# Twelve more weight pieces rounded during attention, the second of an iteration between its halves

## The chip, the cores and the metric

One Trainium2 chip, one core. The metric is the device time of one execution in microseconds (us).

## The reference, cut to what matters

Three layers follow each other: attention with a sigmoid in place of softmax, a mixture of eight experts with one expert for each token, and a gated layer. All of it is float32.

```python
scores = q @ k.T / sqrt(64) - log(448)          # batch 4, 12 heads, 448 tokens, 64 wide
x = sigmoid(scores) @ v                         # -> x [1792, 768]
e = argmax over 8 experts of the logits of x    # gate_w: softmax weight of that expert
x = gate_w * (relu(x @ w1[e]) @ w2[e])          # w1 [8, 768, 1024], w2 [8, 1024, 768]
out = ((x @ w_a) * (x @ w_b)) @ w_out           # 768 -> 1536 -> 768
```

The weights `w_a`, `w_b` and `w_out` of the last layer arrive as float64. The kernel reads each number as two 32-bit words and makes a float32 of them.

## The kernel before

**Precision.** TensorE multiplies in a form that keeps fewer bits than float32, so each operand is split into a high part (a ScalarE cast, L728) and a low part (a VectorE subtraction, L729), and each product takes three matmuls (L1035 to L1037, L1068 to L1070).

**The pieces.** The float64 weights are cut into 72 units (L163): 12 blocks `f` of 128 columns of the middle dimension, three parts (`w_a`, `w_b`, `w_out`), two halves. One unit is 128 x 384 numbers. `prep_load` (L171) issues on the SP queue the load of a unit into a buffer `raw`, of which there are four. `prep_unit` (L185) makes, on VectorE, the upper bits in `m` (L195, L197; two or three buffers), on ScalarE a float of the low word in `raw` itself (L199) and the absolute value of the top 16 bits in `ab` (L201; three buffers), and on GpSimd the sum (L202). `prep_finish` (L205) makes on VectorE the finished number (L212), in `ab` or, in the last layer, in place in the weight buffer. `prep_store` (L221) stores finished units on the SP queue: from `ab` into a scratch tensor `wm` in DRAM (L224).

**The tick.** `prep_tick(dma, behind)` (L226) does one step of this pipeline: store all that is finished, finish all pending units but `behind`, load the unit three ahead, begin the next unit.

**Attention** (L465) has 24 pairs of heads, one for each iteration `i` of the loop at L590 (and one iteration more to drain). In an iteration TensorE transposes q and k of pair i+1 (L515), computes the first half of the scores of pair i (L535, two PSUM buffers), half of the product with v of pair i-1 (L547), the second half of the scores, the second half of the product, and transposes the result of pair i-2 (`x_tok`, L563). ScalarE copies the transposes (L521) and applies the sigmoid from each PSUM buffer (L536). VectorE makes low parts (L522), copies results (L551, L564) and squares (L568). SP issues the loads of q, k (L500) and v (L495) for later pairs near the top of an iteration, and after every third `x_tok` the store of token rows `xs` (L573). In places of the loop `pump` lets the routing of finished batches go on (tables, flags). When the flags of the first half are known, `first_expert` (L794) loads and splits the first expert's weights, one slab in an iteration (L799).

The order on each engine is the order in which the program issues (`manual_schedule`, L1127): every engine and the SP queue work in order, and nothing overtakes. A buffer is given to the next user only when all readers of the former one are done; for `ab` the reader is the store.

Iterations 0 to 2 load a unit each; from iteration 3 on a tick stands at the end of each iteration, and a second one right behind it at iterations 9, 15 and 21: 21 + 3 = 24 units, the blocks 0 to 3 (`F_EARLY = 4`, L164). One of them is stored only in the layer behind, where `first_loads` (L702) drains the pipeline.

**The mixture of experts** (to about 546 us) holds no unit but that drain.

**The last layer** (`glu`, L950) takes the 1792 tokens in groups of 4, 4, 4 and 2 tiles of 128, and for each group goes through the 12 blocks: 48 steps. In a step it splits the weights of the next step (`w_split`, L995), makes both products of the block (`ab`, L1026), copies the first from PSUM (L1040), multiplies (L1043), splits the result, and issues the output matmuls (L1049) of the step before. `w_load` (L982) brings the three parts of a block, 1152 KB, back from `wm` two steps ahead; the blocks from `F_EARLY` on are not loaded in the first group, since `prep_more` (L1084) rounds their units there in place: one tick at the head of a step, one (even steps) or two (odd steps) between its two products, two at its end, as long as the block of the unit is at most 5 ahead of the step (L1088). 48 units are rounded there. At the end of step 1 the tokens of the next group are loaded (L1121).

Of the kernel before, what the change touches and what calls it, by code (L numbers as in the profile page):

```python
# [24 lines left out]
def build(ctx: ExitStack, tc: tile.TileContext, q, k, v, emb, tau, w1, w2, wa, wb, wo, out, dbg=None, stop=None):  # L25
# [6 lines left out]
    nc = tc.nc  # L32
# [128 lines left out]

    HU = DM // 2
    units = [(f, part, hf) for f in range(NF) for part in range(3) for hf in range(2)]  # L163
    F_EARLY = 4  # L164
    next_unit, unit_end = [0], [6 * F_EARLY]
    prep_raw = {}

# [3 lines left out]
    def prep_load(u, dma=nc.sync):  # L171
        if u >= unit_end[0]:
            return
        f, part, hf = units[u]
        t = prep_p.tile([P, HU, 2], I32, tag="raw", name="raw", bufs=4)
        if part < 2:
            src = (wa, wb)[part].bitcast(I32).rearrange("(k p) c -> p k c", p=P)
            dma.dma_start(out=t.rearrange("p (k c) t -> p k (c t)", k=KD // 2),
                          in_=src[:, hf * (KD // 2):(hf + 1) * (KD // 2), 2 * f * P:2 * (f + 1) * P])
        else:  # L180
            src = wo.bitcast(I32).rearrange("(f p) c -> p f c", p=P)
            dma.dma_start(out=t.rearrange("p n t -> p (n t)"), in_=src[:, f, 2 * hf * HU:2 * (hf + 1) * HU])
        prep_raw[u] = t

    def prep_unit():  # L185

        u = next_unit[0]
        if u not in prep_raw:
            return
        next_unit[0] += 1  # L190
        t = prep_raw.pop(u)
        top, low = t[:, :, 1], t[:, :, 0]
        t16 = t.rearrange("p n t -> p (n t)").bitcast(BF16).rearrange("p (n t) -> p n t", t=4)[:, :, 3]
        m = m3[0] if m3 and u % 3 == 2 else prep_p.tile([P, HU], I32, tag="m", name="m", bufs=2)
        nc.vector.tensor_scalar(out=m, in0=top, scalar1=3, scalar2=0x3FFFFFFF,  # L195
                                op0=ALU.logical_shift_left, op1=ALU.bitwise_and)
        nc.vector.scalar_tensor_tensor(out=m, in0=top, scalar=-0x40000000, in1=m,  # L197
                                       op0=ALU.bitwise_and, op1=ALU.bitwise_or)
        nc.scalar.activation(out=low, in_=low.bitcast(U32), func=AF.Copy, scale=2.0 ** -29)  # L199
        ab = prep_p.tile([P, HU], F32, tag="ab", name="ab", bufs=3)  # L200
        nc.scalar.activation(out=ab, in_=t16, func=AF.Abs)  # L201
        nc.gpsimd.tensor_tensor(out=m, in0=m, in1=low, op=ALU.add)  # L202
        prep_sum.append((u, m, ab))

    def prep_finish(behind=0):  # L205

        while len(prep_sum) > behind:
            u, m, ab = prep_sum.pop(0)
            f, part, hf = units[u]
            cs = slice(hf * HU, (hf + 1) * HU)  # L210
            to = wr[f][:, part, cs] if f in wr else ab
            nc.vector.scalar_tensor_tensor(out=to, in0=ab, scalar=1.125 * 2.0 ** -15, in1=m.bitcast(F32),  # L212
                                           op0=ALU.is_ge, op1=ALU.mult)
            if f not in wr:
                prep_out.append((wm_d[f][:, part, cs], ab))
                continue
            wr_n[f] = wr_n.get(f, 0) + 1
            if wr_n[f] == 6:
                prep_out.append((wm_d[f], wr[f]))

    def prep_store(dma=nc.sync):  # L221
        while prep_out:
            o, t = prep_out.pop(0)
            dma.dma_start(out=o, in_=t)  # L224

    def prep_tick(dma=nc.sync, behind=0):  # L226
        prep_store(dma)
        prep_finish(behind)
        prep_load(next_unit[0] + 3, dma)
        prep_unit()  # L230
# [220 lines left out]
    def pump(ps=(True, LATE, END)):  # L451

        while bg:
            job = next((j for j in bg if j[2]), bg[0])
            if job[1] and job[1] not in ps:
                return
            job[2] = False
            try:
                job[1] = next(job[0])
                return  # L460
            except StopIteration:
                bg.remove(job)


    def attention():  # L465
# [16 lines left out]
        NPR = len(pairs)  # L482
# [20 lines left out]
        def tr_pair(i):  # L503

            if i == 1:
                pt = [p.tile([P, 512], F32, tag=t, name=t) for p, t in ((ps_a, "av"), (ps_m, "pm"))]
                parts = [(pt[s][:, :S], slice(s, s + 1)) for s in range(2)]
            else:
                both = ps_t.tile([P, 2, 512], F32, tag="pt", name="pt")
                pt = [both[:, s] for s in range(2)]  # L510
                parts = [(both[:, :, :S], slice(0, 2))]
            for s, nm in enumerate(("q", "k")):
                t = raw.pop((i, nm))
                for c in range(NCH):
                    nc.tensor.transpose(out=pt[s][:, c * CP:(c + 1) * CP], in_=t[:, c].rearrange("p h d -> p (h d)"),  # L515
                                        identity=ident[:CP, :CP])
            hi = qk_p.tile([P, 2, S], F32R, tag="qkh", name="qkh")
            lo = qk_p.tile([P, 2, S], F32R, tag="qkl", name="qkl")
            for src, ss in parts:
                h, l = (t[:, ss, :] if src.ndim == 3 else t[:, ss.start, :] for t in (hi, lo))  # L520
                nc.scalar.copy(out=h, in_=src)  # L521
                nc.vector.tensor_tensor(out=l, in0=src, in1=h.bitcast(F32), op=ALU.subtract)  # L522
            QK[i] = (hi, lo)
# [52 lines left out]
        def routed(b):  # L576
            bg.append([route(b), True, True])
            if b == PHASES[phase_of[b]][-1]:
                bg.append([tables(phase_of[b]), False, False])
# [10 lines left out]
        for i in range(NPR + 1):  # L590
            if 0 < i and i + 1 < NPR:
                tr_pair(i + 1)
            load(i + 3, "qk")
            load(i + 2, "v")
            if i < NPR:
                score_half(i, 0)
            if i == NPR:
                one, turn = misc["ps"], [0]

                def either():  # L600
                    turn[0] ^= 1
                    return ps_s.tile([P, 2, 512], F32, tag="ps", name="pm2")[:, 0] if turn[0] else one()

                misc["ps"] = either
            pump((True,))
            if early_w is None and misc.get("flags0"):
                early_w = first_expert()
            if misc.get("tables0") and not misc.get("gathered"):
                gather(0)
                misc["gathered"] = True  # L610
            if early_w:
                early_w.pop(0)()
            if 1 <= i <= NPR:
                av_part(i - 1, 0)
            pump((True,))
            if i < NPR:
                score_half(i, 1)
            pump((LATE,))
            if 1 <= i <= NPR:
                av_part(i - 1, 1)  # L620
            if i == NPR:
                both = ps_s.tile([P, 2, 512], F32, tag="ps", name="px0")
                x_load(0, [both[:, hf] for hf in range(2)])
                gather(1)
            if i >= 2:
                x_tok(i - 2)
                b, hp = pairs[i - 2]
                if hp == NP - 1:
                    routed(b)
            if i < 3:  # L630
                prep_load(i)
            elif i < NPR:
                prep_tick(nc.sync)
                if i % 6 == 3 and i > 3:
                    prep_tick(nc.sync, 1)
            pump((END,))

        while early_w:
# [155 lines left out]
    def first_expert():  # L794
        e_of[0] = value(0, 2, E - 1, [ET.SP])

        def load(kk):
            if kk < KD:
                nc.sync.dma_start(out=r1[0][:, kk % 2, :], in_=w1[e_of[0], kk * P:(kk + 1) * P, :])  # L799

        def step(kk):
            split(w1h[kk], w1l[kk], r1[0][:, kk % 2, :], w1h[kk].bitcast(F32))
            load(kk + 2)

        load(0)
        load(1)
        return [lambda: None] + [(lambda kk=kk: step(kk)) for kk in range(KD)]
# [142 lines left out]
    def glu():  # L950
# [31 lines left out]
        def w_load(i):  # L982

            if i < len(steps):
                t = w_raw(i)
                if F_EARLY <= i < NF:
                    wraw[i] = [(s, slice(0, DM), t[:, s, :]) for s in range(3)]
# [7 lines left out]
        def w_split(i, parts=range(3), eng=nc.vector):  # L995
            if i < len(steps):
                if parts[0] == 0:
                    wsp[i] = [ws_p.tile([P, 3, DM], F32R, tag=nm, name=nm) for nm in ("whi", "wlo")]
                while F_EARLY <= i < NF and wr_n.get(i, 0) < 6:
                    prep_tick()  # L1000
# [170 lines left out]
```

## Time and profile before

| | us |
|---|---|
| median of three runs | 1116.95 |
| lowest and highest | 1114.82, 1117.33 |
| the profiled execution | 1113.61 |
| its span (first to last instruction) | 1111.9 |
| attention, first score to last product with v | about 10 to 206 |
| last layer, from its first transpose | 546 to 1112 |

The profile is one execution. Busy times are unions of an engine's instructions; TensorE's matmuls are pipelined and overlap. "Idle before" is an engine's gap ahead of an instruction, with the engine or transfer that ended it. PE is TensorE, PEld its weight load, DVE is VectorE, ACT is ScalarE, POOL is GpSimd and SP the queue that issues transfers.

### The profile page before, as it was taken

The numbers are of one execution on the slowest core, as the hardware profiler recorded it, in microseconds if no ns is written. First come the engines' busy times: TensorE is split into PE (matmuls) and PEld (weight loads), VectorE is DVE, ScalarE is ACT, GpSimd is POOL, SyncE is SP. The second block draws the span as 40 slices with busy tenths as digits, with TensorE's granted clock in tenths as the row PEclk, the third lists the DMA queues.
The fourth block names the chain that finished last, engine by engine and source line by source line (L and its number), as shares of the span: only waits on it lengthen the run. The fifth ranks groups of instructions, "written<-read, shape, count | busy, mean of one in ns | idle before, by whom it ended". The sixth has DMA issues, their size and how long they took to land.

```text
span 1111.9 us, 16742 instructions
## 1 busy us (share of the span) xinstructions
PE 1070.6 (96%) x5996; PEld 870.6 (78%) x5996; DVE 603.3 (54%) x1037; ACT 500.3 (45%) x761; POOL 178.2 (16%) x218
## 2 busy tenths in 40 slices
PE   7999999999999999999798889899999999999998
PEld 4555555599989898989787677788888888888997
DVE  2556688864853585352287998643333343333553
ACT  5766767431743474431355556333323232223442
POOL 2121322231221222121123343200000000000000
PEclk9999999999999999999899999999999999999999
DMA  9478586436644775331368566545231072220730
GB/s 201 138 199 214 150 231 197 165 106 266 230 185 169 270 263 192 136 136 45 106 216 278 173 211 214 198 155 214 91 122 43 4 295 103 110 86 1 310 131 29
DMA packets 108681, 182.98 MB, mean 165 GB/s; under 512 B 49560, under 2 KB 80792, under 8 KB 102560
## 3 DMA queue, kind: packets, MB, share of 16 engines
q1 hardware_dynamic: 104608, 166.54, 44.7%
q0 software_dynamic: 3040, 14.94, 3.8%
q8 instruction: 49, 0.80, 0.3%
q14 instruction: 56, 0.46, 0.1%
q10 hardware_dynamic: 928, 0.23, 0.1%
HBM read 149.45 MB, written 32.24 MB: 163 GB/s over the span
## 4 chain that ended last, share of the span: by engine, by line
PE 36%; DVE 9%; DMA 3%; issue 2%; ACT 1%; POOLq 0%; POOL 0%; SPq 0%; ACTq 0%; DVEq 0%
PE ab L1035 8%; PE ab L1037 8%; PE ab L1036 8%; PE o L1068 4%; PE o L1069 4%; PE o L1070 4%; DVE wlo L729 3%; DVE m L195 2%; DVE m L197 1%; DVE wx L212 1%; DMA r<-wm 1%; DMA yg<-ys 1%; DVE r L212 1%; DVE m L1043 1%; DVE gl L729 0%
## 5 line engine op out<-in xcount | busy, mean ns | idle before, releaser
L1035 PE MATMUL ab<-yh,whi 128*128 128x512 f32 (+1 forms) x576 | 211.8, 368 | 17.1 <-DVE m L1043 13.8
L1036 PE MATMUL ab<-yl,whi 128*128 128x512 f32 (+1 forms) x576 | 210.7, 366 | 0.0
L1037 PE MATMUL ab<-yh,wlo 128*128 128x512 f32 (+1 forms) x576 | 210.4, 365 | 0.0
L1035 PEld LDWEIGHTS ab<-yh,whi 128*128 128x128 f32 x576 | 109.7, 190 | 35.2 <-DVE m L1043 15.3
L1037 PEld LDWEIGHTS ab<-yh,wlo 128*128 128x128 f32 x576 | 109.7, 190 | 17.7 <-DVE wlo L729 0.2
L1036 PEld LDWEIGHTS ab<-yl,whi 128*128 128x128 f32 x576 | 109.6, 190 | 16.0
L202 POOL TENSOR_TENSOR m<-m,raw 128x384 int32<-128x384 int32 x72 | 81.8, 1136 | 240.9 <-DVE m L197 77.8
L1068 PE MATMUL o<-whi,gh 128*128 128x512 f32 x336 | 114.7, 341 | 0.0
L1069 PE MATMUL o<-whi,gl 128*128 128x512 f32 x336 | 113.8, 339 | 0.0
L1070 PE MATMUL o<-wlo,gh 128*128 128x512 f32 x336 | 112.9, 336 | 0.0
L536 ACT ACTIVATE a<-ps,bias_s 112x896 f32<-112x896 f32 x96 | 91.6, 1005 | 30.6 <-PE ps L535 30.2
L728 ACT CAST gh<-m 128x512 fp32r<-128x512 f32 (+1 forms) x48 | 27.2, 567 | 169.5 <-DVE m L1043 169.5
L1043 DVE TENSOR_TENSOR m<-ab,a 128x512 f32<-128x512 f32 (+1 forms) x48 | 29.9, 623 | 128.3 <-PE ab L1037 128.3
L729 DVE TENSOR_TENSOR wlo<-r,whi 128x768 fp32r<-128x768 f32 x70 | 65.7, 993 | 45.8 <-ACT whi L728 45.8
L729 DVE TENSOR_TENSOR wlo<-wx,whi 128x768 fp32r<-128x768 f32 x72 | 67.5, 992 | 42.5 <-ACT whi L728 42.5
L790 PE MATMUL p<-w1h,xl 128*128 128x512 f32 x216 | 85.3, 395 | 2.4 <-DVE xl L729 2.4
L788 PE MATMUL p<-w1h,xh 128*128 128x512 f32 x216 | 86.6, 401 | 0.1
L789 PE MATMUL p<-w1l,xh 128*128 128x512 f32 x216 | 84.6, 392 | 0.0
L547 PE MATMUL av<-a,v 112*64 112x448 f32 x384 | 82.5, 551 | 0.0
L874 PE MATMUL p<-w2h,hTh 128*128 128x384 f32 x288 | 76.3, 345 | 0.0
L791 ACT ACTIVATE h<-p 128x512 f32<-128x512 f32 x34 | 20.4, 599 | 123.8 <-PE p L790 123.8
L728 ACT CAST whi<-wx 128x768 fp32r<-128x768 f32 x72 | 55.6, 832 | 42.1 <-PE o L1069 30.2
(224 smaller groups left out, 1894.5 us busy)
## 6 DMA issues: line engine op xcount, KB each, us to landing
wx<-wm SPq DMA_DIRECT2D x20, 1152.0 KB, 9.4
r<-wm SPq DMA_DIRECT2D x19, 1152.0 KB, 6.0
r<-in_moe_w_dram SPq DMA_DIRECT2D x28, 768.0 KB, 8.6
r<-in_moe_w_dram SPq DMA_DIRECT2D x18, 1024.0 KB, 6.3
raw<-in_moe_w_a_dram SPq DMA_DIRECT2D x24, 384.0 KB, 3.4
raw<-in_moe_w_b_dram SPq DMA_DIRECT2D x24, 384.0 KB, 3.5
raw<-in_moe_w_out_dram SPq DMA_DIRECT2D x24, 384.0 KB, 5.4
q<-in_q_dram SPq DMA_DIRECT2D x48, 112.0 KB, 4.3
```

Of the source, the lines that this page charges most:

```text
L536: nc.scalar.activation(out=a[:, c2], in_=ps[:, :, :S], func=AF.Sigmoid, bias=bias_s[:CP], scale=qscale)
L728: nc.scalar.copy(out=hi, in_=src)
L729: eng.tensor_tensor(out=lo, in0=src, in1=f32_hi, op=ALU.subtract)
L788: nc.tensor.matmul(ps, lhsT=xh[:, kk, :], rhs=w1h[kk][:, cs], start=kk == 0, stop=False)
L789: nc.tensor.matmul(ps, lhsT=xh[:, kk, :], rhs=w1l[kk][:, cs], start=False, stop=False)
L790: nc.tensor.matmul(ps, lhsT=xl[:, kk, :], rhs=w1h[kk][:, cs], start=False, stop=kk == KD - 1)
L1035: nc.tensor.matmul(ps[:, :n], lhsT=hi[:, s, cs], rhs=yh[:, kk, :n], start=kk == 0, stop=False)
L1036: nc.tensor.matmul(ps[:, :n], lhsT=hi[:, s, cs], rhs=yl[:, kk, :n], start=False, stop=False)
L1037: nc.tensor.matmul(ps[:, :n], lhsT=lo[:, s, cs], rhs=yh[:, kk, :n], start=False, stop=kk == KD - 1)
L1068: nc.tensor.matmul(t[:, d0:d1], lhsT=gh[:, cs], rhs=hi[:, 2, d0:d1], start=first, stop=False)
L1069: nc.tensor.matmul(t[:, d0:d1], lhsT=gl[:, cs], rhs=hi[:, 2, d0:d1], start=False, stop=False)
L1070: nc.tensor.matmul(t[:, d0:d1], lhsT=gh[:, cs], rhs=lo[:, 2, d0:d1], start=False, stop=last)
```

## The change

`F_EARLY` goes from 4 to 6, so 36 units, the blocks 0 to 5, are rounded before the last layer. The ticks at the ends of iterations stay. The second ticks behind those of iterations 9, 15 and 21 go; in their place a second tick stands between the two halves of an iteration, ahead of the second half's scores, at iterations 4 to 7, 9 to 13, 16 to 19, 22 and 23: 21 + 15 = 36. It leaves one pending unit unfinished (`behind` is 1). In the last layer the blocks 4 and 5 are loaded from `wm` in the first group too (L986), and 36 units are left to round there.

```diff
@@ -161,7 +161,7 @@
-    F_EARLY = 4
+    F_EARLY = 6
     next_unit, unit_end = [0], [6 * F_EARLY]
@@ -613,6 +613,8 @@
             if 1 <= i <= NPR:
                 av_part(i - 1, 0)
             pump((True,))
+            if 3 < i < NPR and (i % 6 not in (2, 3) or i == 9):
+                prep_tick(nc.sync, 1)
             if i < NPR:
                 score_half(i, 1)
             pump((LATE,))
@@ -631,8 +633,6 @@
                 prep_load(i)
             elif i < NPR:
                 prep_tick(nc.sync)
-                if i % 6 == 3 and i > 3:
-                    prep_tick(nc.sync, 1)
             pump((END,))
```

## Rows read from the trace of the kernel before

**Rows 1.** The page: the chain that ended last, its shares by engine

```profile
PE 36%; DVE 9%; DMA 3%; issue 2%; ACT 1%; POOLq 0%; POOL 0%; SPq 0%; ACTq 0%; DVEq 0%
```

**Rows 2.** The chain in order of time: start us, us, what; 564 to 722 us

```profile
564.65 5.52 DMA wx<-wm
...
681.99 0.69 DVE m L1043
...
721.83 0.30 PE o L1068
```

**Rows 3.** Stretches: us, each engine's busy us (instructions), granted clock, DMA share, GB/s

```profile
52.67:60.13 7.46, 7.46 (x53) 4.12 (x53) 4.04 (x10) 5.58 (x7) 1.02 (x1) 1.00 1.05 293
...
101.12:110.40 9.28, 7.79 (x55) 4.06 (x54) 4.13 (x10) 5.95 (x8) 1.02 (x1) 1.00 1.12 283
...
564.70:721.70 157.00, 138.63 (x661) 114.02 (x659) 132.24 (x202) 83.78 (x154) 55.13 (x47) 0.99 0.64 219
721.70:772.00 50.30, 50.30 (x247) 42.46 (x246) 19.19 (x24) 15.93 (x23) 0.00 (x0) 1.00 0.52 204
```

**Rows 4.** Groups of DVE instructions, 564.7 to 699.4 us: busy us, mean ns | idle before

```profile
L195 DVE TENSOR_SCALAR m<-raw 128x384 int32<-128x384 int32 x44 | 32.9, 749 | 1.9 <-DMA raw<-in_moe_w_a_dram 1.9
L197 DVE SCALAR_TENSOR_TENSOR m<-raw,m 128x384 int32<-128x384 int32 x44 | 25.3, 575 | 1.5
L729 DVE TENSOR_TENSOR wlo<-wx,whi 128x768 fp32r<-128x768 f32 x15 | 16.3, 1137 | 2.6 <-ACT whi L728 2.6
...
L212 DVE SCALAR_TENSOR_TENSOR r<-ab,m 128x384 f32<-128x384 f32 x24 | 13.2, 551 | 0.9 <-POOL m L202 0.9
```

**Rows 5.** ACT in order of time, 93 to 106 us: start, us, instruction [idle before]

```profile
97.66 1.91 ACT L536 ACTIVATE a<-ps,bias_s 112x896 f32<-112x896 f32 x2 [1.16 <-PE ps L535]
99.46 0.56 ACT L199 ACTIVATE raw<-raw 128x384 int32<-128x384 uint32 x1
103.38 0.56 ACT L201 ACTIVATE ab<-raw 128x384 f32<-128x384 bf16 x1 [3.37 <-DMA wm<-ab]
```

**Rows 6.** Waits, 20 to 210 us: who for whom: us in total, times, longest

```profile
ACT ab L201 <- DMA wm<-ab: 6.8, 2, 3.4
...
PE ps L535 <- ACT a L536: 3.0, 2, 1.5
```

**Rows 7.** DVE in order of time, around 94 us

```profile
94.18 1.02 DVE L212 SCALAR_TENSOR_TENSOR ab<-ab,m 128x384 f32<-128x384 f32 x2
95.12 0.35 DVE L195 TENSOR_SCALAR m<-raw 128x384 int32<-128x384 int32 x1
95.50 0.56 DVE L197 SCALAR_TENSOR_TENSOR m<-raw,m 128x384 int32<-128x384 int32 x1
```

**Rows 8.** SP's queue in order of time, 93 to 101 us

```profile
93.69 0.58 SPq L573 DMA_DIRECT2D xs<-xtok  x1
...
95.03 2.54 SPq L500 DMA_DIRECT2D q<-in_q_dram  x2
97.66 1.24 SPq L500 DMA_DIRECT2D k<-in_k_dram  x2
98.99 0.56 SPq L495 DMA_DIRECT2D v<-in_v_dram  x1
99.65 0.88 SPq L224 DMA_DIRECT2D wm<-ab  x2
```

**Rows 9.** Transfers by issue, whole span: count, KB each, median us to landing

```profile
wm<-ab SPq DMA_DIRECT2D x24, 192.0 KB, 3.6
```

**Rows 10.** SP's queue: first expert's loads in iterations 18 and 19

```profile
158.82 0.90 SPq L799 DMA_DIRECT2D r<-in_moe_w_dram  x2
...
167.15 0.34 SPq L799 DMA_DIRECT2D r<-in_moe_w_dram  x1
```

**Rows 11.** Stretches as in rows 3: an idle TensorE, and what follows

```profile
663.10:667.50 4.40, 0.01 (x1) 0.01 (x1) 4.27 (x6) 0.58 (x2) 2.31 (x3) 1.00 0.42 135
667.50:677.60 10.10, 10.10 (x39) 8.17 (x40) 8.45 (x14) 8.50 (x16) 4.46 (x4) 0.83 0.61 184
```

## Prediction

> **What bounds the kernel now.** I read the page first, then its chain of waits, then stretches. The chain follows one run of work back from the end; TensorE has 36% of the span in it and DVE 9% [rows 1], and the DVE pieces lie in one place, from the wait for step 2's weights at 565 us to the product of step 8 at 682 us and a little beyond [rows 2]. The stretches [rows 3] say the same: from 721.7 to 772.0 us TensorE is busy all the time and four steps of the last layer take 50.3 us, 12.6 us a step. From 564.7 to 721.7 us, the first eleven steps, it is busy 138.6 of 157.0 us: 18.4 us idle. In this stretch DVE rounds the 48 units that attention left over, beside its own splits. A unit costs DVE the three instructions at L195, L197 and L212, 0.75 + 0.58 + 0.55 = 1.9 us by their means [rows 4]. With four or five of them in a step DVE is later than TensorE, and matmuls at L1035 wait for the product at L1043, which empties the PSUM buffer. So the last layer has at most 18.4 us to give, and only what lies in its first group.
>
> Attention (up to about 206 us) is bound by TensorE: an ordinary iteration, first score to first score, takes 7.46 us and TensorE is busy for all of it [rows 3]. ACT is the engine next to it: it empties the two score buffers with Sigmoids, and TensorE may run two of them ahead, no further. There is a place that shows what happens when ACT is held there: 101.12 to 110.40 us, 9.28 us long, 1.5 us of it idle [rows 3]. ACT stood for 3.4 us at L201, until a store of a rounded unit had landed [rows 5]; it happened twice, and a score matmul waited for ACT 1.5 us each time [rows 6].
>
> **The change, part 1: what attention gains in work.** Twelve more units go through iterations 4 to 23. Each costs DVE 1.5 us there (L195 and L197 0.35 + 0.56, L212 0.55) [rows 4, 7], ACT 1.0 us (L199 and L201, 0.56 each, which overlap a little) [rows 5], GpSimd one addition, SP a load of 384 KB and a store of 192 KB. In an ordinary iteration DVE is busy 4.1 and ACT 5.6 of 7.46 us [rows 3], so the arithmetic fits beside TensorE and costs nothing there. From iteration 17 on DVE is fuller (one-hot tables, first expert's weights), and the two units of iterations 22 and 23 stand closer to the end than the removed second unit of 21: I take 1.5 us for this, between 0 and 4.
>
> **Part 2: the wait between the halves.** This is the term that decides. The buffer `ab` has three copies, so the Abs of unit u (L201) waits until unit u-3 is stored. In an iteration with two ticks the middle tick finishes nothing (one unit pending, behind=1), the end tick finishes both, and the next middle tick stores both and at once takes a unit whose `ab` is the older of these two. So ACT waits for a store that SP gets in the same tick. Counted through the schedule this is so at the middle ticks of iterations 5, 6, 7, 10, 11, 12, 13, 17, 18, 19 and 23; not at 4, 9, 16 and 22. Behind the waiting Abs on ACT stand both Sigmoids of the second half, the two operations of the end tick, the copy of the next transposes and the first Sigmoid of the next iteration.
>
> When does the store land? SP works in order. At the end of iterations 4, 10, 16 and 22 it stands at the store of xs until DVE has copied the last transposes. The trace shows what then follows [rows 8]: xs issued at 93.69, a raw load, two q, two k, one v, and the stores of units at 99.65, although DVE had finished these units at 95.2 [rows 7]. The store lands 3.6 us later [rows 9], so at 103.3, 9.7 us after the first score of that iteration (93.63). Today the Abs stands behind both Sigmoid pairs and the price is 9.28 - 7.46 = 1.8 us. In the changed kernel the same store, at the same place in SP's queue, holds an Abs that stands ahead of the second Sigmoid pair (1.9 us) and of the end tick's two operations (1.0 us) [rows 5]. All that ACT did before the wait it now does after it: 1.8 + 1.9 + 1.0 = 4.7 us for TensorE. Three iterations have it in full, 5, 11 and 17: **14.1 us**. Iteration 23 has no q, k and v loads left ahead of the stores, I take 0.
>
> In iterations 18 and 19 something else stands ahead of the stores on SP: the first expert's loads, which wait for the routing flags (issued at 158.82, 7.4 us into its iteration) and for DVE's split of the first slab (167.15, 6.4 us into its iteration) [rows 10]. That is as late as the 6.0 us above, so the price could be 4.7 us each; but iteration 19 has TensorE work of its own between the halves (9.1 us long), and a stall in 17 lets DVE come earlier with the flags. I take 6 us for both, between 0 and 10.
>
> The others (6, 7, 12, 13): the raw load of an end tick needs the buffer of the middle unit, so SP waits there for the Abs, and the ring closes: raw 0.4, q and k 1.24 each, v 0.56, some 0.2 between, landing 3.6, Abs 0.56 = 7.8 us for 7.46 us of matmuls. That is 0.4 us each, **1.6 us**, between 0 and 7 (a jam like the 2.54 us for q in [rows 8] in each of them). Iteration 10 is longer by its routing work and hides it.
>
> The ticks back to back in 9 and 15 go, and with them the two stalls of [rows 6]: **-3.6 us**. Attention in sum: 14.1 + 6 + 1.6 + 1.5 - 3.6 = **+19.6 us**, with ends +5 and +33.
>
> The landing time is what this hangs on. The Trainium skill (DMA: Bandwidth & Descriptors, Anatomy of one DMA) fits 2.0 us plus bytes over 436 GB/s for one DMA, measured on GpSimd's path: an estimate of 2.5 us for 192 KB, where the trace has 3.6. By it each of the five dear waits would be 1.1 us shorter and attention would lose 14 us. The measured row decides here, as other loads are in front of this store.
>
> **Part 3: the last layer.** Of 48 units 36 are left. The first of them belongs to step 6 and may not start in step 0, so step 0 has none; steps 1 to 7 have four or five as before, step 8 four, 9 and 10 none. On DVE's chain of products (L1043) the first interval loses two units, 3.8 us. Against this the weights of steps 4 and 5 are now loaded (w_load) instead of lying in place. Such a load keeps the split waiting a little: that of step 2 was issued at 564.65 and held ACT until it landed at 570.17 [rows 2]. In all, DVE stood 2.6 us before the splits of such weights, of steps 2 and 3 [rows 4]; the same again, 2.6 us, is given back. So DVE's product of step 8, at 681.99, comes 1.2 us sooner. Behind it is the gain: from there to the output matmuls of 721.83 there were 39.8 us, with seven or eight units in them. Two are left, TensorE leads again, and two and a half steps at 12.6 us are 31.4 us: 8.4 us. In sum **-9.6 us**; at least -4 (the two loads queue behind the 1.5 MB for the next group), at most -18.4, all the idle time.
>
> **The sum**: +19.6 - 9.6 = +10.0 us. The profiled execution took 1113.6 us (span 1111.9); it is 3.3 us under the median of the runs, 1116.95, which I move by the same amount: **1127 us**.
>
> **The rivals.** (a) *The stores land in time.* If SP came to them some 3 us sooner (the xs copy early, no jam), every wait but one would end before ACT is there, since the unit's two operations then fit the gap ahead of the second Sigmoid pair. Attention: 4.7 for one of them + 1.5 + 1 - 3.6 = +3.6; last layer -9.6 to -18: 1102 to 1111, say 1109, faster. For it: ACT has 1.2 us of idle time there [rows 5]. Against it: SP's order is fixed, and [rows 8] are its own times. The point is a landing 5.0 us after the iteration's first score (9.7 - 4.7). Chance 0.17. (b) *Half of it*: 2 us for each dear wait, DVE hidden: attention +9, last layer -9: 1117, the same. Chance 0.12. (c) *Nothing comes back in the last layer* (the DVE chain is refilled by the two loads, -1), or TensorE's clock falls in the new idle times: +19.6 - 1 = 1135 to 1140. The row for the clock: after 4.4 us without work the next 10.1 us had 0.83 of 2.4 GHz granted [rows 11], so part of it at 1.2 GHz, some 1.7 us lost (0.17 x 10.1); a stall here leaves most of its 4.7 us in one idle piece, three to five of them. Against it: after the 1.5 us of today's stall the clock stayed at 1.00. Chance 0.13. The Trainium skill (TensorE: Matmul & The Clock Gate, Part 1) has idle stretches throttle the array to 1.2 GHz until it has been busy again; the trace agrees at [rows 11], and by it case (c) is the one to look for in attention.
>
> **How the numbers follow.** Forecast (ACT held between the halves, 1118 to 1135) 0.58, (a) 0.17, (b) 0.12, (c) 0.13. About 0.2%, 2.2 us, is what a measurement of this kernel can tell from no change. Faster takes (a) and a little of (b): 0.18; same, the rest of (b): 0.10; slower 0.72. The range leaves out the faster half of (a) and the end of (c): 1110 to 1141.
>
> **What would show it.** Right, if the waits list ACT at L201 behind the DMA wm<-ab some ten times with 3 to 6 us at 5, 11 and 17, and TensorE at L535 idle behind L536 for 15 us or more, with iterations of about 12 us at 5, 11, 17; and if from 564 us on the eleven steps take 148 us in place of 157.0. Wrong, if attention still ends near 206 us: then the stores land in time and the last layer alone speaks. Wrong on the last layer, if the product of step 8 is later than today, relative to the first.

## The result and the profile after

| | before | after |
|---|---|---|
| median of eight runs, us | 1115.84 | 1121.9 |
| lowest and highest | 1114.62, 1118.18 | 1118.0, 1124.42 |
| profiled execution, us (span) | 1113.61 (1111.9) | 1118.0 (1116.3) |
| iteration 23 of attention begins | 195.5 | 216.9 |
| first product of the last layer (L1043) | 564.7 | 583.4 |
| from there to the product of step 11 | 157.05 | 142.1 |

The change makes the kernel slower: ratio 1.0053, 95% interval [1.0036, 1.007], some 6 us. Attention loses 21.4 us and the first group of the last layer gains 14.9. (The profiled execution of after is the lowest of its eight, so the two traces are 4.4 us apart in span where the medians are 6 apart.)

The waits of after between 20 and 220 us, as in [rows 6]: who for whom, us in total, times, longest.

```profile
ACT ab L201 <- DMA wm<-ab: 42.1, 13, 7.6
...
PE ps L535 <- ACT a L536: 18.2, 6, 4.4
...
DVE ab L212 <- ACT ab L201: 7.4, 4, 2.7
```

ScalarE's Abs waited for a store 13 times and not twice, and TensorE stood 18.2 us behind the Sigmoids where it had stood 3.0. One more of these waits is listed elsewhere, that of iteration 17:

```profile
162.62 0.54 ACT L201 ACTIVATE ab<-raw 128x384 f32<-128x384 bf16 x1 [6.54 <-DVE ab L212]
```

The view names DVE's instruction because it ended just before, at 162.60. In the program this Abs waits for the store of its buffer, as those of iterations 5 and 11 do, and it starts 3.72 us after that store was issued (158.90), where 5 and 11 have 4.02 and 3.74. So I count it with them; the view alone doesn't show it.

Stretches of after, one iteration each, with the columns of [rows 3]: 5, 6, 7; 11, 12; 17, 18, 19; then the eleven steps from the first product on and the four steps behind them.

```profile
44.85:56.40 11.55, 7.54 (x53) 4.12 (x52) 7.43 (x17) 4.71 (x7) 2.04 (x2) 0.99 0.80 223
56.40:65.29 8.89, 8.89 (x52) 4.89 (x53) 3.71 (x7) 7.31 (x11) 2.04 (x2) 0.82 0.80 230
65.29:72.76 7.47, 7.47 (x53) 4.13 (x53) 5.54 (x13) 5.86 (x9) 2.04 (x2) 1.00 0.84 231
98.80:109.99 11.19, 7.56 (x54) 4.19 (x54) 7.44 (x18) 5.17 (x9) 2.03 (x2) 1.00 0.81 228
109.99:119.26 9.27, 9.24 (x52) 4.62 (x52) 3.71 (x7) 7.75 (x12) 2.04 (x2) 0.82 0.81 236
152.76:164.11 11.35, 7.56 (x54) 4.19 (x54) 10.46 (x25) 4.65 (x7) 4.40 (x8) 1.00 0.85 227
164.11:177.98 13.87, 9.42 (x53) 4.38 (x53) 8.63 (x28) 6.25 (x10) 2.03 (x2) 0.79 0.73 210
177.98:190.56 12.58, 10.68 (x62) 6.11 (x62) 9.30 (x23) 7.23 (x11) 2.04 (x2) 0.82 0.71 207
583.40:725.50 142.10, 136.71 (x661) 114.08 (x659) 114.56 (x170) 74.05 (x134) 41.97 (x36) 0.99 0.59 202
725.50:775.80 50.30, 50.30 (x247) 42.46 (x246) 19.18 (x24) 15.94 (x23) 0.00 (x0) 1.00 0.53 204
```

Length less TensorE's busy time is idle: 4.01 us in iteration 5, 3.63 in 11, 3.79 in 17, 4.45 in 18, 1.90 in 19, together 17.8. But iterations 6 and 12 are long too, and TensorE is busy in them from end to end: their granted clock is 0.82. The same matmuls that take 7.47 us in iteration 7 take 8.89 in 6 and 9.24 in 12, and 18 and 19 run at 0.79 and 0.82 as well. That is 1.4 + 1.8 us and, by an estimate of 0.21 x 9.42 and 0.18 x 10.68, about 2 us each in 18 and 19: some 7 us in all. Idle 18.2 and clock 7, less the 3.7 us by which iterations 12 and 18 of before had been longer: 21.5, the loss of attention. (Iteration 12 took 9.28 us before and takes 9.27 after: then for a stall, now for the clock.)

How one of these iterations comes about is read from SP's queue in iteration 5, as in [rows 8], and from ScalarE beside it, as in [rows 5]:

```profile
44.91 0.62 SPq L573 DMA_DIRECT2D xs<-xtok  x1
45.64 0.56 SPq L182 DMA_DIRECT2D raw<-in_moe_w_out_dram  x1
46.30 2.49 SPq L500 DMA_DIRECT2D q<-in_q_dram  x2
48.88 1.24 SPq L500 DMA_DIRECT2D k<-in_k_dram  x2
50.20 0.56 SPq L495 DMA_DIRECT2D v<-in_v_dram  x1
50.89 0.85 SPq L224 DMA_DIRECT2D wm<-ab  x2
```

```profile
45.83 1.91 ACT L536 ACTIVATE a<-ps,bias_s 112x896 f32<-112x896 f32 x2
47.62 0.56 ACT L199 ACTIVATE raw<-raw 128x384 int32<-128x384 uint32 x1
54.91 0.54 ACT L201 ACTIVATE ab<-raw 128x384 f32<-128x384 bf16 x1 [6.73 <-DMA wm<-ab]
55.36 1.89 ACT L536 ACTIVATE a<-ps,bias_s 112x896 f32<-112x896 f32 x2
```

SP comes to the two stores 6.0 us into the iteration (44.85), the Abs is let go 10.1 us into it, and the Sigmoids of the second half stand behind it.

In the last layer the wait for DVE's product (L1043) is nearly gone. From the first product to that of step 11 TensorE idles 5.4 us (142.10 - 136.71) where it had idled 18.4. The group of the matmuls that follow it, on the page of before, then of after (busy us, mean ns | idle before, what ended most of it), and the shares of the chain after, as in [rows 1]:

```profile
L1035 PE MATMUL ab<-yh,whi 128*128 128x512 f32 (+1 forms) x576 | 211.8, 368 | 17.1 <-DVE m L1043 13.8
```

```profile
PE 39%; DVE 5%; DMA 3%; issue 1%; ACT 1%; POOL 0%; SPq 0%; ACTq 0%
...
L1035 PE MATMUL ab<-yh,whi 128*128 128x512 f32 (+1 forms) x576 | 210.0, 365 | 2.2 <-DVE m L1043 2.1
```

The idle time goes from 17.1 to 2.2 us, and DVE's share of the chain from 9 to 5%.

### The profile page after: what moved, and what is told of

Its sections match the earlier page's. It is cut to its first block, busy times and chain, and to the rows that moved or that the text cites. A ratio compares the mean times of both kernels' runs of the same rounds, so it can differ in the third digit from the quotient of the medians.

```text
span 1116.3 us, 16783 instructions
## 1 busy us (share of the span) xinstructions
PE 1073.7 (96%) x5996; PEld 871.1 (78%) x5996; DVE 598.3 (54%) x1037; ACT 497.9 (45%) x761; POOL 175.4 (16%) x218
## 5 line engine op out<-in xcount | busy, mean ns | idle before, releaser
L1035 PE MATMUL ab<-yh,whi 128*128 128x512 f32 (+1 forms) x576 | 210.0, 365 | 2.2 <-DVE m L1043 2.1
L1035 PEld LDWEIGHTS ab<-yh,whi 128*128 128x128 f32 x576 | 108.8, 189 | 18.6 <-DVE m L1043 2.6
L1043 DVE TENSOR_TENSOR m<-ab,a 128x512 f32<-128x512 f32 (+1 forms) x48 | 29.9, 623 | 136.1 <-PE ab L1037 136.1
L547 PE MATMUL av<-a,v 112*64 112x448 f32 x384 | 87.8, 582 | 0.0
L728 ACT CAST whi<-r 128x768 fp32r<-128x768 f32 x70 | 53.8, 831 | 47.2 <-PE o L1069 39.9
```

Of the source, the lines that this page charges most:

```text
L547: nc.tensor.matmul(t[j * D:(j + 1) * D, :S], lhsT=raw[i, "v"][:, j, c, :], rhs=a[:, c2, j, :], start=c == 0, stop=c == NCH - 1)
L1035: nc.tensor.matmul(ps[:, :n], lhsT=hi[:, s, cs], rhs=yh[:, kk, :n], start=kk == 0, stop=False)
```

## The experiments

The theory (A): the Abs between the halves reuses a buffer whose store was issued only in the same iteration, behind q, k and v, and this wait is all that attention loses; a copy more, or an earlier store, gives it back. The rival (B): the twelve units fill ScalarE, DVE or the queue, or the clock falls, so that attention stays long whatever the store does. Times are medians; each ratio is to runs of the kernel before beside it. A difference in us is one of medians, if not said to go by the ratio.

### Six copies of `ab` in attention

Three more buffers, in a pool (`misc["ab"]`) that is open during attention alone.

```diff
-        ab = prep_p.tile([P, HU], F32, tag="ab", name="ab", bufs=3)
+        more = misc.get("ab") if u < 33 and u % 6 >= 3 else None
+        ab = (more.tile([P, HU], F32, tag="ab2", name="ab", bufs=3) if more
+              else prep_p.tile([P, HU], F32, tag="ab", name="ab", bufs=3))
```

> The changed kernel, with six copies of `ab` in attention in place of three (three more in a pool of attention's own), so the Abs of unit u waits for the store of unit u-6, which was issued two iterations earlier. Theory A (the wait for the store between the halves is the loss): the waits of ACT L201 behind wm<-ab (42 us in the changed kernel) go, the 18 us of TensorE waiting for ACT at L535 and the slow clock after them go too; attention ends about 3 us after that of the kernel before or earlier, and with the 15 us that the last layer gives the time is 1100 to 1106 us. Rival B (the added arithmetic and the added 6.9 MB of transfers are the loss): attention stays some 20 us longer, 1117 to 1122 us.

1101.35 us, ratio 0.985 [0.9824, 0.9875]: 20.5 us under after, and under before as well. Iterations 5 to 7 and 11 to 13 take 7.5 us each, and iteration 23 begins at 195.9, as in before. A single Abs still waits for a store, in iteration 23 (TensorE idles 1.4 us behind it):

```profile
ACT ab L202 <- DMA wm<-ab: 3.4, 1, 3.4
```

Ahead of that, one stretch is left in which TensorE idles, at iterations 17 to 19 (19 takes 13.5 us, against 9.1 in before):

```profile
160.00:180.00 20.00, 17.62 (x110) 9.48 (x108) 16.96 (x40) 12.07 (x17) 3.08 (x3) 0.91 1.05 301
```

There TensorE waits for DVE's one-hot tables, and behind that its clock falls (0.91 over these 20 us). DVE is busy for 17 of them; it was so in before too (17.12), so its share alone doesn't tell that it is late:

```profile
PE pm L428 <- DVE hotb L411: 2.4, 2, 1.7
```

A holds for everything but this: elsewhere twelve units and their transfers lie in attention without being seen.

### Stores ahead of the loads

After, with the three copies it has, and one line at the top of an iteration:

```diff
+            prep_store()
             load(i + 3, "qk")
             load(i + 2, "v")
```

> The changed kernel, three copies of `ab`, xs in its place; the stores of finished units are issued at the top of each iteration, ahead of the q, k and v loads, in place of the middle tick. SP then stands until DVE has finished the units (about 1.5 us into the iteration) and the store lands about 5 us into it, before the first expert's loads too. If SP's order is what makes the stores late: no iteration over 9.2 us but 19 (DVE's tables), waits of ACT behind wm<-ab from 42 us to under 15, 1100 to 1106 us. If only moved, as in the run that moved xs: the loads of q, k and v come late and the wait turns up there, 1112 to 1120 us.

1102.38 us, ratio 0.9864 [0.9834, 0.9893], as good as the three further copies. Iteration 5, SP and ScalarE:

```profile
45.45 0.56 SPq L182 DMA_DIRECT2D raw<-in_moe_w_out_dram  x1
46.11 2.24 SPq L224 DMA_DIRECT2D wm<-ab  x2
48.45 1.67 SPq L500 DMA_DIRECT2D q<-in_q_dram  x2
```

```profile
51.46 0.57 ACT L201 ACTIVATE ab<-raw 128x384 f32<-128x384 bf16 x1 [3.48 <-DMA wm<-ab]
```

The stores are issued at 46.11 and no longer at 50.89, and the Abs starts 3.5 us sooner. The waits in the stretch of attention:

```profile
ACT ab L201 <- DMA wm<-ab: 19.9, 10, 3.7
...
PE ps L535 <- ACT a L536: 2.6, 3, 1.0
```

The Abs still waits 19.9 us, more than the 15 that I expected at most, but TensorE stands behind the Sigmoids for 2.6 us and not 18.2, and iteration 5 takes 8.31 us, 17 8.51. (19, with 12.21, is the one over 9.2 us that isn't so long in before.) So a wait of 3.5 us costs 0.8 and one of 6.7 us costs 4.1: of each wait TensorE doesn't feel the first 2.6 us or so.

### The two halves of the change, each alone

Last layer alone: attention and its 24 units as before, but blocks 4 and 5 read from `wm`, where they find the numbers of blocks 0 and 1 (the rounding of blocks 4 and 5 is left out). Attention alone: 36 units as after, and all blocks from 4 on rounded again in the last layer as before.

```diff
-    F_EARLY = 4
-    next_unit, unit_end = [0], [6 * F_EARLY]
+    F_EARLY, F_ATT = 6, 4                           # attention alone: 4, 6
+    next_unit, unit_end = [0], [6 * F_ATT]
...
-                    nc.sync.dma_start(out=t, in_=wm_d[steps[i][1]])
+                    nc.sync.dma_start(out=t, in_=wm_d[steps[i][1] - 4 if 4 <= steps[i][1] < 6 else steps[i][1]])
...
         unit_end[0] = len(units)
+        next_unit[0] = 6 * F_EARLY
```

> Attention as in the kernel before (24 units), the last layer as in the changed kernel (36 units left). The units 24 to 35 are rounded nowhere; the loads of blocks 4 and 5 read the scratch of blocks 0 and 1 instead, of the same size. It gives the last layer's gain by itself. As read from the trace of the changed kernel: 157.0 to 142 us for the eleven steps, so 1100 to 1104 us in all. By the sum that was forecast: -9.6 us, 1106 to 1108.

> Attention as in the changed kernel (36 units), the last layer as in the kernel before: it begins at block 4 again, so the units 24 to 35 are rounded twice. It gives attention's loss by itself. Theory A and the trace of the changed kernel: +21 us, 1134 to 1140 us. If attention's loss were made up later (a shift that the expert layer hides), under 1130.

The last layer alone: 1101.92 us, ratio 0.9864 [0.9837, 0.9892], -14.6 us. Attention alone: 1138.57, ratio 1.018 [1.0153, 1.0207], +22 us. The sum, +7.4, is near the +6 of the whole change. The stretch from the first product to that of step 11, first in the one, then in the other (157.00 before [rows 3], 142.10 after):

```profile
564.55:707.62 143.07, 137.43 (x661) 115.07 (x659) 114.64 (x170) 74.06 (x134) 41.68 (x36) 0.98 0.59 199
```

```profile
588.76:747.13 158.37, 141.06 (x661) 116.13 (x659) 132.38 (x203) 83.89 (x154) 54.85 (x47) 0.97 0.65 217
```

The halves don't touch each other: each stretch goes with its own last layer. How much clock a stall costs isn't fixed, though. In the trace of attention alone iteration 6 takes 10.38 us at 0.70, where after, with the same instructions, has 8.89 at 0.82; its iteration 23 begins 3.2 us later than that of after.

### One block fewer in the last layer

As the last layer alone, but with `F_EARLY` 5: block 5 is rounded there.

> Attention as in the kernel before (24 units), the last layer with one block (six units) fewer to round in place of two; the units 24 to 29 are rounded nowhere, the load of block 4 reads the scratch of block 0. In the kernel before the head of steps 6, 7 and 8 takes a unit more than its schedule, since the block it splits is not yet done; with one block fewer none does. If these forced units and the end of the chain are what the last layer loses, one block brings most of the 14.6 us of two: 9 to 13 us, 1104 to 1108. If the gain goes by the number of units: half, 7 us, 1109 to 1110.

1110.39 us, ratio 0.9939 [0.9918, 0.9961]: -5.5 us, or -6.8 by the ratio, close to half of the two blocks' -14.6 (-15.2 by the ratio) and less than I had expected. In its trace the eleven steps are only 3.8 us shorter. The intervals between successive products (us), worked out from the starts of L1043, and under them the units begun in each (L195):

```
before     14.97 13.45 16.06 12.42 14.91 12.90 17.36 15.24 17.36 10.50 11.88   157.05
               5     4     5     4     5     4     6     5     6     2     0
one block  14.70 13.10 18.89 12.41 14.93 12.90 15.06 12.90 14.81 10.91 12.67   153.28
               5     4     5     4     5     4     5     4     4     0     0
after       9.50 12.79 16.49 12.77 15.04 12.89 15.05 12.89 10.32 11.70 12.66   142.10
               3     4     5     4     5     4     5     4     2     0     0
```

Between the fourth interval and the eighth one with four units takes 12.4 to 12.9 us, near TensorE's own pace of 12.6 [rows 3]; five take about 15.0, six 17.4. So there each unit beyond four costs some 2.4 us. (The first three hold waits for loads too, and the last ones the end of the rounding: four units took 14.81 in the ninth with one block.) In before the seventh to the ninth interval hold 6, 5 and 6 units, one each more than the ticks of `prep_more` give. By this count they belong to the heads of steps 7 to 9, not 6 to 8 as I had written. They come from `w_split` (L999): where a block's units aren't begun when it is to be split, it ticks there and then, and with `behind` 0, so that DVE has to wait for GpSimd. Such a tick in before, with DVE in order of time:

```profile
655.34 0.55 DVE L212 SCALAR_TENSOR_TENSOR r<-ab,m 128x384 f32<-128x384 f32 x1
656.81 0.56 DVE L212 SCALAR_TENSOR_TENSOR r<-ab,m 128x384 f32<-128x384 f32 x1 [0.92 <-POOL m L202]
657.29 0.36 DVE L195 TENSOR_SCALAR m<-raw 128x384 int32<-128x384 int32 x1
```

Already one block fewer takes these ticks away (-7.2 us in three intervals), but 2.8 us are lost again at the third interval and 1.2 in the last two. In the third ScalarE waits for the load of block 4, which lay in place in before:

```profile
603.50 2.30 ACT L728 CAST whi<-r 128x768 fp32r<-128x768 f32 x3 [2.99 <-DMA r<-wm]
```

### The second tick behind the second half's scores

```diff
-            if 3 < i < NPR and (i % 6 not in (2, 3) or i == 9):
-                prep_tick(nc.sync, 1)
             if i < NPR:
                 score_half(i, 1)
+            if 3 < i < NPR and (i % 6 not in (2, 3) or i == 9):
+                prep_tick(nc.sync, 1)
             pump((LATE,))
```

> The changed kernel with the middle tick moved behind the scores of the second half, so that on ACT both Sigmoids of that half stand ahead of the Abs; the number of units, copies, stores and the order on SP stay. Theory A: the price of a dear wait falls by the 1.9 us of these Sigmoids, from about 4 us to 2, and with shorter idle times TensorE's clock falls less: 6 to 12 us sooner than the changed kernel, 1110 to 1116 us. Rival B: the place on ACT is of no matter, 1118 to 1124.

1118.63 us, ratio 1.0015 [0.9995, 1.0034]: only 3 us under after, not the 6 to 12 expected. Iterations 5 to 7, 12 with its part behind the idle piece, then 18 and 19:

```profile
45.24:52.72 7.48, 7.48 (x53) 4.18 (x52) 5.62 (x13) 5.22 (x7) 1.99 (x2) 1.00 0.79 208
52.72:63.13 10.41, 7.80 (x53) 4.06 (x52) 5.51 (x13) 6.43 (x9) 2.09 (x3) 1.00 0.82 235
63.13:72.03 8.90, 7.80 (x53) 4.05 (x52) 5.51 (x13) 6.43 (x10) 2.04 (x2) 1.00 0.85 227
105.72:117.59 11.87, 9.36 (x53) 4.63 (x52) 5.51 (x13) 7.96 (x12) 2.02 (x2) 0.86 0.81 235
111.33:117.59 6.26, 6.23 (x32) 3.17 (x32) 2.21 (x6) 4.77 (x7) 1.14 (x2) 0.73 0.87 240
158.60:168.95 10.35, 7.80 (x53) 4.05 (x53) 9.19 (x28) 6.38 (x9) 2.64 (x5) 1.00 0.71 200
168.95:186.15 17.20, 11.55 (x62) 6.87 (x61) 9.89 (x24) 7.41 (x10) 2.92 (x3) 0.80 0.79 234
```

The dear wait now leaves 2.5 to 2.6 us of idle in one piece. In iteration 6 it costs 2.9 us and no clock (1.00 in 6 and 7), but in 12 the clock falls behind 2.5 us of idle (0.73), and that iteration takes 4.4 us more than 7.5. Up to the beginning of iteration 19 this kernel is 9.0 us ahead of after (168.95 against 177.98), as much as was expected of it. In iteration 19 a second way to the end opens, and 19 and 21 (17.20 and 11.63 us, against 12.58 and 9.40) take most of it back. In 19 the Abs waits 7.2 us for a store behind the first expert's loads, DVE has to finish that unit before anything else in its order, and the one-hot tables for the routing come behind it; TensorE's loads of them stood idle for up to 6.0 us:

```profile
DVE ab L212 <- ACT ab L201: 10.3, 5, 4.7
PEld pm L427 <- issue: 6.7, 2, 6.0
```

That the tables are late for DVE's wait I read from the order in the program; "issue" in this row names no releaser. What is measured is that the place in the iteration shortens each stall, and that as long as the store is late most of this is lost again.

### The store of xs later

After, with the xs store of the first half of a batch (L573) issued behind the next middle tick, so that SP doesn't stand at it.

> The changed kernel, three copies of `ab`, with one thing moved on SP: the store of xs that follows the third `x_tok` of a batch (end of iterations 4, 10, 16, 22) is issued behind the middle tick of the next iteration, so that it no longer stands ahead of the q, k, v loads and of the stores of units. If SP's wait at xs is what makes the stores of iterations 5, 11 and 17 late: these iterations fall from 11.2 to 11.6 us to under 8.5 (the ring of loads, stores and Abs at 7.8 us), the slow clock behind them goes, while 18 and 19 (first expert's loads) stay: 10 to 14 us sooner than the changed kernel, 1107 to 1112 us. If the stores are late for another reason (landing time, DVE): no change, 1118 to 1124.

1117.09 us, ratio 1.0006 [0.999, 1.0022], 4.8 us under after and not the 10 to 14 expected. Iterations 5, 11 and 17 fall to 7.5 us, as they should without the copy that SP waits for. But 6 and 12 stay long (9.2 and 9.1 us), 7, 9 and 13 rise from 7.5 to 8.2, 8.2 and 8.4, 18 from 13.9 to 16.9 and 20 from 9.4 to 11.0; 19 stays at 12.8. The wait of iteration 5 has moved on by one iteration, to the middle tick of 6:

```profile
60.40 0.55 ACT L201 ACTIVATE ab<-raw 128x384 f32<-128x384 bf16 x1 [4.36 <-DMA wm<-ab]
```

The store that it waits for was issued at 55.54, in the same tick again. SP shows what follows: the raw load of the end tick wants the buffer that this Abs still has to read, stands for it (4.9 us for the two raw loads), and q and k queue behind it.

```profile
56.52 4.87 SPq L178 DMA_DIRECT2D raw<-in_moe_w_b_dram  x2
61.48 1.23 SPq L501 DMA_DIRECT2D q<-in_q_dram  x2
```

So xs decides which iteration is hit first, not whether one is. What makes the later ones (18 and 20) longer than in after I have not followed up.

### Four copies, and six with an earlier choice of iterations

> The changed kernel with four copies of `ab` in attention (one more). The Abs of unit u then waits for the store of unit u-4, which was issued one iteration earlier, not in the same tick. Theory A says that one copy more is enough: waits of ACT L201 behind wm<-ab near zero, 1100 to 1104 us as with six copies. If the stores were late by more than an iteration, it would lie between: 1106 to 1115.

1107.64 us, ratio 0.9923 [0.99, 0.9946]: one copy more is not enough. Waits are left, now at the end ticks, whose unit follows by four one that was stored in the same iteration's middle tick, so I had counted wrongly; 5 waits, 18.9 us, the longest 6.9:

```profile
ACT ab L202 <- DMA wm<-ab: 18.9, 5, 6.9
```

In iteration 6 TensorE idles only 1.7 us behind one of them, and its clock falls all the same (from the end of that piece to the end of the iteration); behind 1.6 us in iteration 12 it doesn't (1.00):

```profile
57.93:64.22 6.29, 6.25 (x32) 3.13 (x32) 2.21 (x6) 3.96 (x6) 1.02 (x1) 0.73 1.02 241
```

Six copies, and the second ticks at iterations 4 to 16, 22 and 23, none where DVE is full:

```diff
-            if 3 < i < NPR and (i % 6 not in (2, 3) or i == 9):
+            if 3 < i < 17 or 21 < i < NPR:
```

> Six copies of `ab` and the fifteen second ticks at iterations 4 to 16, 22 and 23, none at 17 to 21. With six copies one iteration alone was longer than in the kernel before, iteration 19 with 13.5 us against 9.1, where a matmul waited for DVE's one-hot tables. If DVE, filled by the units of 17 to 19, is the cause: iteration 19 back at 9.1 and 3 to 5 us sooner than with six copies alone, 1096 to 1099 us. If not: 1101 again.

**1096.07 us**, ratio 0.9824 [0.9802, 0.9845], faster than either kernel. Iteration 19 takes 9.1 us again, and the stretch that was left with six copies alone is now full:

```profile
160.00:180.00 20.00, 20.00 (x138) 11.29 (x138) 17.26 (x40) 14.61 (x19) 2.39 (x3) 1.00 1.03 293
```

### The kernel before with six copies

> The kernel before (24 units) with six copies of `ab` in attention. Its two stalls behind the back-to-back ticks go (iterations 12 and 18, 9.3 us each, back to 7.5) and a smaller one in 22: 3 to 4 us sooner than the kernel before, 1111 to 1113 us. Attention should then end where that of the changed kernel with six copies and early second ticks ends (iteration 23 begins at 191 to 192 us in its trace): twelve more units would cost attention nothing but a wait. If the stalls had been paid back elsewhere, no change: 1115 to 1117.

1111.12 us, ratio 0.9955 [0.9939, 0.9971]: -5 us by the ratio (-6 by the medians). The two stalls of [rows 6] go (iterations 12 and 18 take 7.49), and iteration 23 begins at 192.3. With the 36 units of the kernel just above it begins at 191.6: with the wait out of the way, the twelve further units cost attention nothing. The ratio of the two kernels, 0.9824 / 0.9955 = 0.987, is that of the last layer alone, 0.986.

## Why the prediction was right and wrong

**Direction and mechanism: right.** The forecast case, ScalarE held between the halves, is what the trace shows, and three copies more or one line on SP take it away: +6 us against a forecast of +10, inside the range. What rival (a), stores in time, would have given, the store-first kernel shows: 1102.4, the lower end of its 1102 to 1111.

**The landing (part 2): right to 0.4 us.** Forecast 9.7 us into the iteration by [rows 8, 9], measured 10.1. The stores were issued at 50.89 and the Abs let go 4.0 us later; by the 2.5 us that the prediction estimated from the Trainium skill (DMA: Bandwidth & Descriptors, Anatomy of one DMA) the wait would have been shorter by 1.5, and the trace doesn't agree with it for a store behind other loads.

**The price of a dear wait: 2.5 us low in sum, by two errors against each other.** Forecast 4.7 us for each of 5, 11 and 17, 14.1 in all. TensorE stood 4.0, 3.6 and 3.8, 11.4 in all: it starts again (56.40 in iteration 5) behind the first Sigmoid that follows the Abs (55.36), and the end tick's two operations, which the forecast counted with 1.0 us, come only at 57.14. What followed wasn't in this term: the next iteration at a clock of 0.79 or 0.82, some 5.2 us more. The prediction had the row for that [rows 11], and left it to rival (c) with 0.13, on the strength of a 1.5 us stall that had cost no clock; its own forecast of 4.7 us in one piece is nearer to the 4.4 us of [rows 11] and should have carried that row's 1.7 us three to five times. Measured 1.4 to 2.0 in four places. The rule cited there (the Trainium skill, TensorE: Matmul & The Clock Gate, Part 1) agrees with these rows (0.79 to 0.82); shorter pauses went both ways (last section).

**Iterations 18 and 19: low.** Forecast 6 us, measured 6.4 us idle and 1.9 us of clock in 19; the 2.0 in 18 follow the stall of 17 and are counted there.

**The closed ring (6, 7, 12, 13): too high.** Forecast 1.6 us, measured none: 7 and 13 take 7.5 us, and 6 and 12 are long for the clock alone. Where the store of xs is later, iterations 7 and 9 do take 8.2 us; that a ring closes there is what I read from SP's queue, and no run shows it by itself.

**Work and removed stalls: about right.** 1.5 us were allowed for the arithmetic. The kernels without the wait show 0 with the early choice and, with the change's own choice of iterations, an iteration 19 longer by 4.4 us. The removed stalls were put at -3.6; the two iterations had been 3.7 longer, and the kernel before gains 5 (by the ratio) without its stalls.

In sum attention lost 21.4 us in the trace (22 alone) against a forecast of 19.6. That these are so close is in part luck: the ring and the work, 3.1 us that were not there, made up for most of the clock that was missing.

**The last layer: the step that failed.** Forecast -9.6, measured -14.9 (-14.6 alone). The prediction said that steps 1 to 7 have four or five units "as before" and let the product of step 8 come 1.2 us sooner relative to the first; it came 9.9 us sooner (107.4 us behind it, 117.3 before). Three terms of that were mis-sized. The forced ticks of `w_split` in before weren't counted: without them two intervals shrink by 2.3 us each. The first interval is 5.5 us shorter and not 3.8: it begins two units fewer, but of the three that it begins only one is finished (L212) in it, where before five were. DVE is busy 8.50 us in place of 13.30, the third number of busy time here:

```profile
564.68:579.65 14.97, 14.97 (x73) 12.61 (x72) 13.30 (x20) 8.17 (x15) 5.54 (x5) 1.00 0.60 210
583.42:592.92 9.50, 9.50 (x45) 7.93 (x44) 8.50 (x12) 6.07 (x11) 2.25 (x2) 1.00 0.23 66
```

And the loads of steps 4 and 5 gave back 0.8 us (third and fourth interval), not 2.6; this one differs from run to run (1.6 in the last layer alone, 2.8 for the one load with one block). Behind step 8 it was the other way round, 5.1 us in place of 8.4: TensorE is busy for all of the 34.7 us that are left there, where the forecast had counted 31.4.

So in the traces +10.0 became +4.4 us: the last layer gave 5.3 more than forecast, and 2.7 came back ahead of it (below); against that attention cost 1.8 more, and 0.6 were lost behind step 11, which was not forecast.

**Open.** The first product of after comes 18.7 us later than before's, where iteration 23 had begun 21.4 later. The first matmuls at L1035 ran at a higher granted clock in after (0.90 from 567.0 to 583.4, against 0.73 from 546.0 to 564.7 before), but attention alone has 0.82 there and no such gain. In the kernel with six copies that stretch has 0.91, yet its first product comes 369.4 us behind the beginning of iteration 23, as in before (369.2; after 366.5). No run tells which of this is the change's doing.

## What to carry to other kernels

Where a step moves within a loop that keeps engines in order, count which use of a buffer it takes over and where, in the order of the issuing queue, the release of that use stands; the arithmetic may be free and the place not. To the idle time of a stall add the clock of the stretch behind it, where the trace has a row for such a pause. Then look at the queue before the schedule: here one line of issue order, or three buffers, were worth more than the place of the tick (some 20 us against 3).

## What the runs showed of the hardware

- Behind idle pieces of TensorE of 3.6 to 4.4 us the next iterations had a granted clock of 0.79 to 0.82, so part of them ran at 1.2 and not 2.4 GHz; 0.70 in iteration 6 of attention alone, behind 4.3 us. Shorter pieces went both ways: behind 2.6 us (second tick behind the scores, iteration 6), 1.6 us (four copies, iteration 12) and 1.5 us (before, iteration 12) the clock stayed at 1.00, behind 2.5 us (second tick behind the scores, iteration 12) and 1.7 us (four copies, iteration 6) it fell to 0.73 for the rest of the iteration. So the length of the pause alone doesn't tell whether the clock falls.
- Issues on SP are not of one length. The two loads of q took 2.49 us behind xs and a raw load, and 1.23 behind raw loads alone (store of xs later). With the stores put first, it was the stores behind xs and the raw load that took 2.24 in place of 0.85 us, and q then 1.67. In these rows the delay, 1.3 to 1.4 us, fell on what came second behind xs; what makes it isn't shown.
